# Two steps' 64-row low products on the two halves of the array's rows, in the kernel of an attention and two feed-forward networks

## The chip, the core and the metric

The kernel runs on one core of a Trainium2 chip. TensorE (PE in the rows) multiplies, its weight loads (PEld) stand apart from its matmuls; VectorE is DVE, ScalarE is ACT, GpSimd is POOL, SyncE (SP) issues transfers. The metric is the device time of one execution in microseconds. Before the change the median of three runs is 1066.04 us (1063.58 to 1072.04).

## The reference

Three stages follow each other. The first is a recurrence over 768 steps for 4 x 8 heads of width 40; its output, 3072 rows of 320 numbers, goes through a network of 8 experts (one expert a row, a hidden layer of 1024, relu) and a second network with one set of weights (a hidden layer of 2048, elu). The change touches the two networks alone:

```python
    h = np.maximum(np.einsum('ecd,edf->ecf', disp, w1), 0.0)
    y = np.einsum('ecf,efd->ecd', h, w2)
    ...
    out[i] = gate_w[i] * y[expert_idx[i], pos[i]]
```

```python
    h = x @ w_in
    alpha = 1.0
    g = np.where(h > 0.0, h, alpha * (np.exp(np.minimum(h, 0.0)) - 1.0))
    return (g @ w_out).astype(np.float32)
```

## The kernel before, in words

Every float32 operand of the networks is split into a high part, rounded to the format fp32r, and a low part, what the rounding left. A product is the sum of high by high, low by high and high by low. The input has 320 rows (the contraction), in three pieces of 128, 128 and 64.

A *block* is a set of tokens: 8 blocks of 448 columns for the experts (class `Turned`), then 6 blocks of 512 for the second network (class `Sorted`). A block runs over *steps*, each 128 hidden units: 8 steps for an expert, 16 for the second network, so 64 + 96 = 160 steps in all. In step f the method `s1` makes the hidden layer's product in one bank of PSUM (`ph`) by eight matmuls (L968). Six of them take the pieces of 128 rows: the high and the low weights by the high input `XH`, the high weights by the low input `XL`. The last two take the 64-row piece from the tile `XS`, which has the high input in partitions 0 to 63 and the low input in 64 to 127. The weights of these 64 rows lie twice, in the upper and in the lower partitions, so the high weights `ha` by XS give high by high and high by low at once. The low weights `la` by XS give low by high and, beside it, low by low.

Then `s2` makes the second layer's product of an earlier step (three steps back for an expert, four for the second network) in the banks `po`: 8 matmuls of 448 columns, or 12 of 320 (L992 to L994). After that the activation of the step runs on ACT, DVE and POOL, in two parts that lie a step apart: relu (L1097, L1098), or elu (L1104 to L1112), whose last reader of the bank ph is L1110 on DVE. `run` writes this order out: s1, s2, the activation's parts, a part of the preparation of the next block, then the splitting of weights four groups of steps ahead (ACT L775, POOL L780) and, during the experts, the conversion of the second network's weights on DVE (L858 to L870).

The pool of the banks ph has four buffers, which the transposes of the next expert's input (`pt`) share. `prep` makes XH, XL and XS of the next block: for experts from transposes in PSUM (L952, L953), for the second network from the loaded rows (L1061, L1062). The last step of an expert writes its output through the tile `half`.

Of the kernel before, what the change touches and what calls it, by code (L numbers as in the profile page):

```python
# [8 lines left out]
F32 = mybir.dt.float32  # L9
F32R = mybir.dt.float32r  # L10
# [12 lines left out]
SL = 448  # L23
# [862 lines left out]
def ffn(tc, nc, cst, disp, xt, w1, w2, w32, out, ring, W0, cv):  # L886
# [3 lines left out]
    ap = ctx.enter_context(tc.tile_pool(name="fa", bufs=2))  # L890
    dr = ctx.enter_context(tc.tile_pool(name="fdr", bufs=1, space=DRAM))
    gp = ctx.enter_context(tc.tile_pool(name="fg", bufs=1))
    ps = ctx.enter_context(tc.tile_pool(name="fps", bufs=4, space=PSUM))
# [11 lines left out]
    class Block:  # L905
# [31 lines left out]
        def parts(s):  # L937
            s.XH = ap.tile([128, 2, 512], F32R, tag="XH", name="XH")
            s.XL = ap.tile([128, 2, 512], F32R, tag="XL", name="XL")
            s.XS = ap.tile([128, 512], F32R, tag="XS", name="XS")  # L940
            return [((s.XH[:, k] if k < 2 else s.XS[0:64])[:, 0:s.T], (s.XL[:, k] if k < 2 else s.XS[64:128])[:, 0:s.T]) for k in range(3)]

        def prep(s, P=None):
            for k, (h, l) in enumerate(s.parts()):
                w = (128, 128, 64)[k]
                if P:
                    p = P[k]
                else:
                    p = ps.tile([128, 512], F32, tag="ph", name="pt")
                    for i in range(4):  # L950
                        s.turn(p, i, k)
                nc.scalar.copy(h, p[0:w, 0:s.T])  # L952
                nc.vector.tensor_tensor(l, p[0:w, 0:s.T], h.bitcast(F32), op=ALU.subtract)  # L953
                if k == 2:
                    s.keep(p)
                yield

# [2 lines left out]

        def s1(s, f):
            ha, la, _, _ = s.W.ab(f)
            p = ps.tile([128, 512], F32, tag="ph", name="ph")
            seq = [(w[:, k], x[:, k]) for w, x in ((ha, s.XH), (la, s.XH), (ha, s.XL)) for k in (0, 1)]
            seq += [(ha[:, 2], s.XS), (la[:, 2], s.XS)]
            p = p[:, 0:s.T]
            for i, (l, r) in enumerate(seq):
                nc.tensor.matmul(p, l, r[:, 0:s.T], start=i == 0, stop=i == len(seq) - 1)  # L968
            H = ap.tile([128, 512], F32R, tag="H", name="H", bufs=6)[:, 0:s.T]
            L = ap.tile([128, 512], F32R, tag="L", name="L", bufs=6)[:, 0:s.T]  # L970
            return p, H, L
# [4 lines left out]
        def s2(s, f, HL):  # L976
            if f == 0:
                s.po = s.bank(4)
            for i in range(4):
                s.part(i, f, HL)  # L980
            if f == s.W.nf - 1:
                s.out()
                for i in range(4):
                    s.evict(i)
# [29 lines left out]
    class Turned(Block):  # L1014
# [8 lines left out]
        def s2(s, f, HL):  # L1023
            _, _, hb, lb = s.W.ab(f)
            _, H, L = HL
            if f == 0:
                s.po = s.bank(3)
            first, last = f == 0, f == s.W.nf - 1
            p0, p1, p2 = (p[:, 0:SL] for p in s.po)
            a, b, c = (slice(128 * k, min(128 * k + 128, D)) for k in range(3))  # L1030
            nc.tensor.matmul(p0, hb[:, a], H, start=first, stop=False)
            nc.tensor.matmul(p1, hb[:, b], H, start=first, stop=False)
            nc.tensor.matmul(p0, lb[:, a], H, start=False, stop=False)
            nc.tensor.matmul(p1, lb[:, b], H, start=False, stop=False)
            if not last:
                nc.tensor.matmul(p2, s.W.tail(f), H, start=first, stop=False)
            nc.tensor.matmul(p0, hb[:, a], L, start=False, stop=last)
            nc.tensor.matmul(p1, hb[:, b], L, start=False, stop=last)
            nc.tensor.matmul(p2[0:64], hb[:, c], L, start=False, stop=False)
            if last:  # L1040
                nc.tensor.matmul(p2, s.W.tail(f), H, start=False, stop=True)
                Y, half = s.Y, ap.tile([64, SL], F32, tag="half", name="half", bufs=1)
                if s.G is None:
                    nc.scalar.copy(Y[:, 0], p0)  # L1044
                    nc.vector.tensor_copy(Y[:, 1], p1)
                    nc.scalar.copy(half, p2[64:128])
                    nc.vector.tensor_tensor(Y[0:64, 2], p2[0:64], half, op=ALU.add)
                else:
                    nc.scalar.copy(half, p2[64:128])
                    nc.vector.tensor_tensor(Y[:, 0], p0, s.G, op=ALU.mult)  # L1050
                    nc.vector.tensor_tensor(Y[:, 1], p1, s.G, op=ALU.mult)
                    nc.vector.tensor_tensor(half, p2[0:64], half, op=ALU.add)
                    nc.vector.tensor_tensor(Y[0:64, 2], half, s.G[0:64], op=ALU.mult)
                s.store(Y)

    class Sorted(Block):

        def prep(s, P=None):
            for k, (h, l) in enumerate(s.parts()):
                x = s.X[0:(128, 128, 64)[k], k]  # L1060
                nc.scalar.copy(h, x)  # L1061
                nc.vector.tensor_tensor(l, x, h.bitcast(F32), op=ALU.subtract)  # L1062
                yield

    def soft(s, tag="s"):
# [48 lines left out]
    def gates():  # L1114

        OH = cst["oh"]
        T = lambda nm, sh, dt=F32: gp.tile(sh, dt, tag="g" + nm, name=nm, bufs=1)
        for nm in ("blk", "tmo", "l1"):
            cst[nm] = T(nm, [128, 128], BF)
        set_gates(nc, cst)  # L1120
        m = T("m", [128, 2, 8, 12])
        nc.vector.memset(m, 1.0)
        nc.vector.memset(m[:, :, :, 0:1], 0.0)
        ic = T("ic", [128, 2, 8, 12], BF)
        nc.vector.tensor_tensor_scan(
            out=ic.rearrange("p b e c -> p (b e c)"), data0=m.rearrange("p b e c -> p (b e c)"),
            data1=OH.rearrange("p b e c -> p (b e c)"), initial=0.0, op0=ALU.mult, op1=ALU.add)
        S = T("S", [128, 2, 8], BF)
        nc.vector.tensor_copy(S, ic[:, :, :, 11])
        p = ps.tile([128, 512], F32, tag="ph", name="pg")  # L1130
        p1 = p[:, 0:192]
        nc.tensor.matmul(p1, cst["tmo"], OH.rearrange("p b e c -> p (b e c)"), start=True, stop=False)
        nc.tensor.matmul(p1, cst["blk"], ic.rearrange("p b e c -> p (b e c)"), start=False, stop=True)
        nc.tensor.matmul(p[:, 192:208], cst["l1"], S.rearrange("p b e -> p (b e)"), start=True, stop=False)
        nc.tensor.matmul(p[:, 200:208], cst["ones"], S[:, 0], start=False, stop=True)
        b = T("b", [128, 2, 8])
        nc.vector.tensor_copy(b.rearrange("p b e -> p (b e)"), p[:, 192:208])
        t = T("t", [128, 2, 8, 12])
        nc.vector.tensor_tensor(t, p1.rearrange("p (b e c) -> p b e c", b=2, e=8),
                                b.unsqueeze(3).to_broadcast([128, 2, 8, 12]), op=ALU.add)  # L1140
        nc.vector.scalar_tensor_tensor(out=t, in0=t, scalar=over["cap"], in1=OH, op0=ALU.is_lt, op1=ALU.mult)
        kp = T("kp", [128, 24])
        nc.vector.tensor_reduce(kp.rearrange("p (c b) -> p b c", b=2), t.rearrange("p b e c -> p b c e"), axis=AX.X, op=ALU.add)
        eb0 = T("eb0", [128, 8])
        nc.vector.tensor_scalar(eb0, cst["ebase"], float(-SL), None, op0=ALU.add)
        nc.vector.tensor_tensor(t, OH, eb0.unsqueeze(1).unsqueeze(3).to_broadcast([128, 2, 8, 12]), op=ALU.mult)
        eb = T("eb", [128, 24])
        nc.vector.tensor_reduce(eb.rearrange("p (c b) -> p b c", b=2), t.rearrange("p b e c -> p b c e"), axis=AX.X, op=ALU.add)
        pos, epos = T("pos", [128, 24]), T("epos", [128, 24])
        nc.vector.tensor_tensor(pos, cst["slot"], eb, op=ALU.subtract)  # L1150
        nc.vector.tensor_scalar(pos, pos, float(-SL), None, op0=ALU.add)
        nc.vector.scalar_tensor_tensor(out=epos, in0=eb, scalar=1.0 / 8, in1=pos, op0=ALU.mult, op1=ALU.add)
        return kp, pos, epos
# [205 lines left out]
    def overflow():  # L1359
# [6 lines left out]
        with tc.For_i(1, nr, 1) as r:  # L1366

            kp, pos, epos = gates()
            zr = ap.tile([128, 512], F32, tag="M", name="M")[:, 0:RW]
            nc.vector.memset(zr, 0.0)  # L1370
# [44 lines left out]
    start = over["start"] = ap.tile([128, 6], F32, name="begin", bufs=1)  # L1415
# [72 lines left out]
```

## Time and profile before

| | before |
|---|---|
| median of 3 runs | 1066.04 us |
| the profiled execution: time, and span | 1064.33 us, 1062.6 us |
| granted TensorE clock, mean | 0.941 of full |
| PE busy | 965.8 us (91%), 9995 matmuls |
| PEld busy | 871.9 us (82%) |
| DVE, ACT, POOL busy | 727.8, 516.9, 606.5 us |
| chain that ended last | PE 28%, issue 10%, POOL 6%, DVE 6%; its largest line PE ph L968, 14% |

The attention takes the first 453 us, the experts run to about 690 us, the second network from there on. A row of a timeline gives the start of a group, how long it lasted, the engine, the line, the operation with the tile written and the tiles read, then for PE the rows and columns of the array that it uses (64*64 is a quarter), the operand's shape and the count. Matmuls are pipelined, and their ends are modelled: the time from one start to the next tells what each costs, and the recorded length holds a constant tail. In the rows, fp32r operands are named f32.

### The profile page before, as it was taken

To read this page: it belongs to the slowest core of one execution; us is meant where nothing else is said; L and a number is where in the kernel's file an instruction comes from. 1 tells how busy PE (TensorE), PEld (TensorE's weight loads), DVE (VectorE), ACT (ScalarE), POOL (GpSimd) and SP (SyncE) were. 2 spreads that over 40 slices of the span, in tenths; PEclk is the share of its full clock that TensorE was granted. 3 is DMA by queue.
4 is the path that set the end of the run, shared out by engine and by line. 5 is a ranking of instruction groups with operands and counts; after the bars stand their busy time and mean duration, and the time that the engine had idled before them with its cause. 6 is when DMAs were issued, how large, how long until landed. Compare 5 with 4: busy or idle time off the path is not lost.

```text
span 1062.6 us, 25351 instructions
## 1 busy us (share of the span) xinstructions
PE 965.8 (91%) x9995; PEld 871.9 (82%) x9995; DVE 727.8 (68%) x1287; ACT 516.9 (49%) x1011; POOL 606.5 (57%) x926
## 2 busy tenths in 40 slices
PE   5869978899899999888999999989999999999993
PEld 4758877798788889677889888869989989989983
DVE  8856756788674677549798963656766767776751
ACT  4646544556463334244535545454555455554551
POOL 4757839899898813456677876733323333323332
PEclk9866988899899889999999999989999999999997
DMA  6768675667654864576877765400101010100000
GB/s 165 163 179 197 168 137 105 151 131 141 139 110 103 192 164 103 155 203 168 230 218 209 221 193 188 161 23 3 48 1 32 19 26 25 26 25 1 26 1 28
DMA packets 180984, 121.67 MB, mean 115 GB/s; under 512 B 105792, under 2 KB 166872, under 8 KB 179224
## 3 DMA queue, kind: packets, MB, share of 16 engines
q1 hardware_dynamic: 176788, 102.89, 39.6%
q0 software_dynamic: 3168, 11.14, 3.0%
q10 hardware_dynamic: 900, 5.93, 2.2%
q8 instruction: 81, 1.33, 0.6%
q14 instruction: 47, 0.39, 0.1%
HBM read 86.87 MB, written 33.05 MB: 113 GB/s over the span
## 4 chain that ended last, share of the span: by engine, by line
PE 28%; issue 10%; POOL 6%; DVE 6%; DMA 4%; ACT 2%; SPq 1%; POOLq 0%; DVEq 0%; ACTq 0%
PE ph L968 14%; PE po L992 4%; PE po L994 4%; PE po L993 4%; POOL ring L780 3%; POOL L L1112 2%; DMA ring<-in_w_dram 2%; DVE L L1098 1%; ACT ring L775 1%; SPq L801 1%; DMA S<-in_w_in_dram 1%; DMA w<-E 1%; POOL out_dram L1282 1%; DVE E L859 1%; DVE M L867 1%
## 5 line engine op out<-in xcount | busy, mean ns | idle before, releaser
L780 POOL TENSOR_TENSOR ring<-ring,ring 128x64 fp32r<-128x64 f32 (+2 forms) x320 | 195.7, 647 | 90.0 <-ACT ring L775 87.7
L1112 POOL TENSOR_TENSOR L<-E,H 128x512 fp32r<-128x512 f32 x66 | 87.6, 1327 | 185.8 <-ACT H L1111 148.2
L968 PE MATMUL ph<-XH,ring 128*128 128x512 f32 (+1 forms) x640 | 172.9, 392 | 4.4 <-DVE L L1098 3.9
L968 PEld LDWEIGHTS ph<-XH,ring 128*128 128x128 f32 x640 | 117.4, 193 | 19.6 <-DVE L L1098 4.5
L1105 ACT ACTIVATE E<-N 128x512 f32<-128x512 f32 x96 | 60.7, 633 | 143.7 <-DVE N L1104 88.0
L992 PE MATMUL po<-ring,H 128*128 128x320 f32 x384 | 119.6, 311 | 5.5 <-ACT Y L1044 5.3
L353 POOL TENSOR_TENSOR X<-X,ring 128x60 f32<-128x60 f32 (+19 forms) x170 | 114.9, 676 | 13.3
L994 PE MATMUL po<-ring,L 128*128 128x320 f32 x384 | 119.6, 311 | 1.5 <-POOL L L1112 1.5
L993 PE MATMUL po<-ring,H 128*128 128x320 f32 x384 | 119.4, 311 | 0.0
L1104 DVE TENSOR_SCALAR N<-ph 128x512 f32<-128x512 f32 x96 | 65.9, 686 | 47.4 <-PE ph L968 47.0
L968 PE MATMUL ph<-XL,ring 128*128 128x512 f32 (+1 forms) x320 | 97.6, 386 | 0.0
L968 PE MATMUL ph<-XS,ring 128*128 128x512 f32 (+1 forms) x320 | 97.5, 386 | 0.0
L351 POOL TENSOR_TENSOR ring<-X,ring 128x60 f32<-128x60 f32 (+19 forms) x108 | 74.2, 687 | 39.0 <-DMA ring<-dab 18.2
L992 PEld LDWEIGHTS po<-ring,H 128*128 128x128 f32 x384 | 72.6, 189 | 10.5 <-ACT Y L1044 5.7
L993 PEld LDWEIGHTS po<-ring,H 128*128 128x128 f32 x384 | 72.7, 189 | 4.1
L994 PEld LDWEIGHTS po<-ring,L 128*128 128x128 f32 x384 | 72.9, 190 | 2.0 <-POOL L L1112 2.0
L1109 DVE SCALAR_TENSOR_TENSOR M<-E,M 128x512 f32<-128x512 f32 x96 | 70.7, 736 | 5.5 <-ACT M L1106 5.5
L775 ACT CAST ring<-ring 128x704 fp32r<-128x704 f32 x80 | 61.4, 779 | 21.3 <-issue 8.2
L1110 DVE SCALAR_TENSOR_TENSOR E<-ph,M 128x512 f32<-128x512 f32 x96 | 66.4, 691 | 7.8
L968 PEld LDWEIGHTS ph<-XL,ring 128*128 128x128 f32 x320 | 61.1, 191 | 10.8
L968 PEld LDWEIGHTS ph<-XS,ring 128*128 128x128 f32 x320 | 60.8, 190 | 10.8
L1111 ACT CAST H<-E 128x512 fp32r<-128x512 f32 x96 | 59.2, 617 | 15.1 <-DVE E L1110 12.0
(238 smaller groups left out, 2164.2 us busy)
## 6 DMA issues: line engine op xcount, KB each, us to landing
ring<-in_w_dram SPq DMA_DIRECT2D x16, 640.0 KB
ring<-in_w_dram SPq DMA_DIRECT2D x32, 256.0 KB
RVU<-in_d_in_dram SPq DMA_DIRECT2D x48, 160.0 KB
dab<-AB SPq DMA_DIRECT2D x24, 256.0 KB
ring<-in_e_in_dram ACTq DMA_DIRECT2D x18, 321.6 KB
ring<-w SPq DMA_DIRECT2D x4, 1408.0 KB
disp<-ring SPq DMA_DIRECT2D x8, 575.8 KB
ring<-in_w_dram SPq DMA_DIRECT2D x32, 128.0 KB
```

The lines of the kernel that those rows point to most:

```text
L351: nc.gpsimd.tensor_tensor(tv, X[:, 0:n, s:s + 1].to_broadcast([128, n, m]), N[:, s:s + 1, s + 1:e].to_broadcast([128, n, m]), op=ALU.mult)
L353: nc.gpsimd.tensor_tensor(X[:, 0:n, s + 1:e], X[:, 0:n, s + 1:e], tv, op=ALU.subtract)
L775: s.nc.scalar.copy(B[:, 0:704], r)
L780: s.nc.gpsimd.tensor_tensor(B[:, to], r[:, q], B[:, q].bitcast(F32), op=ALU.subtract)
L968: nc.tensor.matmul(p, l, r[:, 0:s.T], start=i == 0, stop=i == len(seq) - 1)
L992: nc.tensor.matmul(o, H[:, c], hb, start=f == 0, stop=False)
L993: nc.tensor.matmul(o, H[:, c], lb, start=False, stop=False)
L994: nc.tensor.matmul(o, L[:, c], hb, start=False, stop=f == s.W.nf - 1)
L1104: nc.vector.tensor_scalar(N, p, 0.0, None, op0=ALU.min)
L1109: nc.vector.scalar_tensor_tensor(out=M, in0=E, scalar=1.0, in1=M, op0=ALU.add, op1=ALU.mult)
L1110: nc.vector.scalar_tensor_tensor(out=E, in0=p, scalar=0.0, in1=M, op0=ALU.max, op1=ALU.add)
L1112: eng.tensor_tensor(L, E, H.bitcast(F32), op=ALU.subtract)
```

## The change

For each pair of steps (f even, f + 1) `s1` takes both banks ph at the beginning of the even step. The low weights' product of the 64-row piece is no longer a matmul of full height in each step. In the even step the matmul L973 takes the upper 64 partitions alone (low weights by the high input, without low by low), and right behind it L974 does the same for the next step, on the lower 64 partitions, with that step's low weights and a second copy of the high input, `XD`, which stands in partitions 64 to 127. L974 opens the bank of the odd step, whose `s1` then has seven matmuls. `prep` gets one copy more on ACT for XD. To make room for XD, `half` moves into a buffer of the tile N, and a tile t of the gates (run only when an expert overflows) into the tile m.

```diff
             s.XS = ap.tile([128, 512], F32R, tag="XS", name="XS")
+            s.XD = ap.tile([128, 512], F32R, tag="XD", name="XD")
...
                 if k == 2:
+                    nc.scalar.copy(s.XD[64:128, 0:s.T], p[0:64, 0:s.T])
                     s.keep(p)
...
             ha, la, _, _ = s.W.ab(f)
-            p = ps.tile([128, 512], F32, tag="ph", name="ph")
+            if f % 2 == 0:
+                s.ph = [ps.tile([128, 512], F32, tag="ph", name="ph")[:, 0:s.T] for _ in range(2)]
+            p = s.ph[f % 2]
             seq = [(w[:, k], x[:, k]) for w, x in ((ha, s.XH), (la, s.XH), (ha, s.XL)) for k in (0, 1)]
-            seq += [(ha[:, 2], s.XS), (la[:, 2], s.XS)]
-            p = p[:, 0:s.T]
+            seq += [(ha[:, 2], s.XS)]
             for i, (l, r) in enumerate(seq):
-                nc.tensor.matmul(p, l, r[:, 0:s.T], start=i == 0, stop=i == len(seq) - 1)
+                nc.tensor.matmul(p, l, r[:, 0:s.T], start=f % 2 == 0 and i == 0, stop=f % 2 == 1 and i == len(seq) - 1)
+            if f % 2 == 0:
+                nc.tensor.matmul(p, la[0:64, 2], s.XS[0:64, 0:s.T], start=False, stop=True)
+                nc.tensor.matmul(s.ph[1], s.W.ab(f + 1)[1][64:128, 2], s.XD[64:128, 0:s.T], start=True, stop=False)
...
-                Y, half = s.Y, ap.tile([64, SL], F32, tag="half", name="half", bufs=1)
+                Y, half = s.Y, ap.tile([128, 512], F32, tag="N", name="N")[0:64, 0:SL]
...
+                if k == 2:
+                    nc.scalar.copy(s.XD[64:128], x)
...
-        t = T("t", [128, 2, 8, 12])
+        t = T("m", [128, 2, 8, 12])
```

What this does to the order on TensorE is shown at two places. The first is the beginning of the first expert, steps 0 and 1, before the change (ph is the hidden layer's bank, ring_5566 the weights):

```order
L968 MATMUL ph<-XH,ring_5566 128x448 x4
L968 MATMUL ph<-XL,ring_5566 128x448 x2
L968 MATMUL ph<-XS,ring_5566 128x448 x2
L968 MATMUL ph<-XH,ring_5566 128x448 x4
L968 MATMUL ph<-XL,ring_5566 128x448 x2
L968 MATMUL ph<-XS,ring_5566 128x448 x2
```

And the same two steps after it:

```order
L971 MATMUL ph<-XH,ring_5566 128x448 x4
L971 MATMUL ph<-XL,ring_5566 128x448 x2
L971 MATMUL ph<-XS,ring_5566 128x448
L973 MATMUL ph<-XS,ring_5566 128x448
L974 MATMUL ph<-XD,ring_5566 128x448
L971 MATMUL ph<-XH,ring_5566 128x448 x4
L971 MATMUL ph<-XL,ring_5566 128x448 x2
L971 MATMUL ph<-XS,ring_5566 128x448
```

The even step has kept eight matmuls and got a ninth, which belongs to the odd step; the odd step has seven. The second place is an even step of the second network with the beginning of the s2 that follows it (po is an output bank), before and then after the change:

```order
L968 MATMUL ph<-XH,ring_8868 128x512 x4
L968 MATMUL ph<-XL,ring_8868 128x512 x2
L968 MATMUL ph<-XS,ring_8868 128x512 x2
L992 MATMUL po<-ring_8793,H 128x320
L993 MATMUL po<-ring_8793,H 128x320
L994 MATMUL po<-ring_8793,L 128x320
```

```order
L971 MATMUL ph<-XH,ring_8886 128x512 x4
L971 MATMUL ph<-XL,ring_8886 128x512 x2
L971 MATMUL ph<-XS,ring_8886 128x512
L973 MATMUL ph<-XS,ring_8886 128x512
L974 MATMUL ph<-XD,ring_8886 128x512
L998 MATMUL po<-ring_8811,H 128x320
L999 MATMUL po<-ring_8811,H 128x320
L1000 MATMUL po<-ring_8811,L 128x320
```

L973 and L974 stand between the last full-height matmul of s1 and the first of s2 (L998, which was L992). The order on the other engines is as it was, with the copy XD added on ACT behind the cast of XS.

## Rows read from the trace of the kernel before

**Rows 1.** Windows by stage: length, busy us by engine (count), clock, DMA, GB/s.
```profile
core 0: us, PE busy (x) PEld busy (x) DVE busy (x) ACT busy (x) POOL busy (x), PEclk, DMA share, GB/s
453.00:709.00 256.00, 238.58 (x1167) 209.98 (x1166) 179.60 (x323) 125.05 (x231) 175.70 (x286) 0.97 0.65 187
709.00:1062.60 353.60, 337.07 (x1865) 303.62 (x1863) 229.14 (x335) 174.56 (x304) 115.83 (x117) 0.98 0.06 20
```
**Rows 2.** Waits of PE, 453 to 709 us: total us, times, longest us.
```profile
PE po L992 <- ACT Y L1044: 5.3, 1, 5.3
PE ph L968 <- DVE L L1098: 3.9, 2, 3.4
PE po L1031 <- DVE Y L1050: 2.6, 1, 2.6
```
**Rows 3.** Waits of PE, 709 us to the end.
```profile
PE po L994 <- POOL L L1112: 1.5, 2, 0.8
```
**Rows 4.** Timeline of PE in a step of the second network.
```profile
803.87 0.63 PE L968 MATMUL ph<-XS,ring 128*128 128x512 f32 x2
804.34 0.30 PE L992 MATMUL po<-ring,H 128*128 128x320 f32 x1
```
**Rows 5.** Timeline of PE in a step of an expert.
```profile
562.33 0.58 PE L968 MATMUL ph<-XS,ring 128*128 128x448 f32 x2
562.75 0.36 PE L1031 MATMUL po<-H,ring 128*128 128x448 f32 x1
```
**Rows 6.** Timeline of PEld, the load ahead of that L992.
```profile
804.11 0.19 PEld L992 LDWEIGHTS po<-ring,H 128*128 128x128 f32 x1
```
**Rows 7.** Timeline of PE and PEld, 314.60 to 314.63 us: full height to quarters.
```profile
314.41 0.28 PE L525 MATMUL q<-RVU 128*128 128x128 f32 x1
314.62 0.27 PE L469 MATMUL ut<-TT,RH 64*64 64x64 f32 x2
314.62 0.14 PEld L469 LDWEIGHTS ut<-TT,RH 64*64 64x64 f32 x2
```
**Rows 8.** The same, 315.72 to 315.75 us: quarters to full height.
```profile
315.54 0.22 PE L469 MATMUL ut<-TT,RH 64*64 64x64 f32 x2
315.70 0.38 PE L525 MATMUL q<-RVU 128*128 128x128 f32 x1
315.70 0.19 PEld L525 LDWEIGHTS q<-RVU 128*128 128x128 f32 x1
```
**Rows 9.** The same, 151.955 to 151.97 us: rows change, columns don't.
```profile
151.75 0.28 PE L469 MATMUL ut<-TT,RH 64*64 64x64 f32 x4
151.96 0.14 PEld L539 LDWEIGHTS y<-RVU,SD 128*64 128x64 f32 x2
```
**Rows 10.** The same, 560.42 to 560.52 us: columns change, rows don't.
```profile
560.30 0.36 PE L1038 MATMUL po<-L,ring 128*128 128x448 f32 x1
560.31 0.14 PEld L1039 LDWEIGHTS po<-L,ring 128*64 128x64 f32 x1
```
**Rows 11.** Timeline of PE, quarters in pairs and halves by columns.
```profile
314.62 1.15 PE L469 MATMUL ut<-TT,RH 64*64 64x64 f32 x32
318.21 1.10 PE L539 MATMUL y<-RVU,SD 128*64 128x128 f32 x16
```
**Rows 12.** Groups by line and shape, PE: count, busy us, mean ns, idle before.
```profile
L968 PE MATMUL ph<-XS,ring 128*128 128x512 f32 x192 | 60.5, 396 | 0.0
L968 PE MATMUL ph<-XS,ring 128*128 128x448 f32 x128 | 37.0, 371 | 0.0
```
**Rows 13.** The same, ACT, 453 to 1062 us.
```profile
L1061 ACT CAST XS<-X 64x512 fp32r<-64x512 f32 x6 | 3.7, 616 | 0.0
```
**Rows 14.** Timeline of DVE at two places.
```profile
477.44 0.43 DVE L858 TENSOR_SCALAR N<-S 128x512 int32<-128x512 int32 x1 [7.41 <-DMA S<-in_w_in_dram]
797.05 0.69 DVE L1110 SCALAR_TENSOR_TENSOR E<-ph,M 128x512 f32<-128x512 f32 x1
```
**Rows 15.** Timeline of PE, end of the s1 three steps later.
```profile
800.25 0.62 PE L968 MATMUL ph<-XS,ring 128*128 128x512 f32 x2
```

## The prediction

> **What bounds the kernel now.** I read the table of windows first, then the waits of the tensor engine, then single matmuls. The change touches only the two networks, which run from about 453 us to the end. There the matmul engine is busy 238.6 of 256.0 us and 337.1 of 353.6 us [rows 1], and its waits name little else: the longest of the expert stage is 5.3 us, once, the next 3.9 us in two [rows 2]; the third stands at 2.6 us, and from 709 us on there is 1.5 us in all, at the very end [rows 2, 3]. So every tenth of a microsecond that a step gains or loses on this engine shows in the time nearly whole, in the second network above all.
>
> A step of the second network gives 0.47 us to its last two matmuls, the two on XS: 803.87 to 804.34, so 0.235 us each [rows 4]. In an expert the two take 562.33 to 562.75, 0.21 us each [rows 5]. Each also needs a load of weights; but the load for the next matmul starts at 804.11 [rows 6], as soon as the matmul ahead of it (803.87 + 0.235) has begun, and so lies wholly beside it. That is the cover to keep in mind.
>
> **What goes and what comes.** Two steps now have four XS matmuls of full height; afterwards they have two of full height and two of 64 rows, L973 and L974, which are meant to run side by side. There are as many instructions as before: 192 XS matmuls of 512 columns (2 for each of 96 steps) and 128 of 448 (64 steps) [rows 12]. If a pair took the time of one matmul and nothing else happened, 48 pairs x 0.225 and 32 x 0.20 would go (0.01 us for the later start of the second): 10.8 + 6.4 = 17.2 us.
>
> **Do two halves run together?** The attention has pairs on opposite quarters of the array. Their records start together (the two of "314.62 0.27 x2" share a start), and 32 of them, 16 pairs, span 1.15 us, against 1.10 us for 16 matmuls twice as wide [rows 7, 11]. So yes for quarters that share neither rows nor columns. The new pair shares all 128 columns and writes two banks; no row shows that. Bounds: 0.01 us for the second, or its whole slot (0.235 and 0.21). I take 0.01, since the nearest rows are of that kind.
>
> **What the change of height costs.** Here the rows speak against the change. The last full-height matmul ahead of such quarters starts at 314.41 and is recorded for 0.28; the first load of quarter size starts only at 314.62, 0.07 before that recorded end, not 0.01 after the matmul's start as usual [rows 7]. On the way back it is the same: last quarters at 315.54 for 0.22, the next load at 315.70, 0.06 before their end [rows 8]. Where only the rows change (64 high and 64 wide to 128 high and 64 wide) it stays: 151.75 + 0.28, less 151.96, is 0.07 [rows 9]. Where only the columns change, 128 wide to 64 wide, the load follows its matmul at once, 560.30 and 560.31 [rows 10]. Nor is a semaphore the likely cause: the lag is the same 0.06 to 0.07 at all three places, whoever produces the next operand. So a change of the number of rows empties the engine, and the loads behind it lose their cover: the first full matmul after it is recorded for 0.38 instead of 0.28, 0.10 us in which its weights arrive; for quarters it is 0.27 against 0.22, 0.05 [rows 7, 8].
>
> The Trainium skill, TensorEngine Tiling (Array Packing), section Tiling Modes, says the same: a change of the tiling mode, not just of the tile, drains the engine. It gives no figure; the trace agrees with it by the 0.07 and 0.10 above.
>
> Now the sum for two steps, from the start of the last full-height XS matmul of the even step. At 512 columns a matmul is recorded for 0.40 (0.63 for two, less 0.235) [rows 4]: load at 0.40 - 0.07 = 0.33, stream from 0.43, second half 0.01 later, load of the next full matmul 0.33 after that at 0.77, its stream at 0.87. Before, that stream began at 0.47. So the even step loses 0.40, the odd one, an XS matmul shorter, gains 0.235: a loss of 0.165 a pair, 48 x 0.165 = 7.9 us. At 448 columns (recorded 0.37): 0.30, 0.40, 0.41, 0.71, 0.81 against 0.42 [rows 5]; 0.39 - 0.21 = 0.18 a pair, 32 x 0.18 = 5.8 us. Together 13.7 us more.
>
> Bounds: the first load has half the rows, so its uncovered part may be 0.05 as for quarters: 80 x 0.05 = 4.0 less. The lag I read to 0.02, twice a pair: 3.2 either way.
>
> **What hides some of it.** In the second network no wait is left to take it up. In the experts there is. At 477.44 VectorE gets a transfer after 7.41 us of idleness [rows 14], and the tensor engine's longest wait on VectorE's L (3.4 of the 3.9) hangs on that; what is late by less before it costs nothing: steps 0, 2, 4 and 6, four pairs. The waits of 2.6 and 5.3 us should swallow some seven more. 11 x 0.18 = 2.0 us less; the bounds are 0 and all 5.8. I take 2.0, because the other waits follow chains that the tensor engine's own steps feed, so they move along.
>
> **The rest.** The bank of an odd step is opened a half step earlier, so its last reader must be done earlier. In the second network the reader of three steps ahead ends at 797.05 + 0.69 = 797.74, and the place of the new L974 is 800.25 + 0.235 = 800.49: 2.7 us of room [rows 14, 15]. So nothing; without this room each pair would wait. The low weights that L974 takes belong to the next step of the same group and are split by POOL well ahead. The copy XD is one more cast of the size of XS's (0.616 us in each of the 6 blocks of the second network, and one for each of the 8 experts) [rows 13]; ACT is busy 125 of 256 us and 175 of 354 us [rows 1], and the copy is needed only a step later: nothing; if it had to be waited for, 14 x 0.6 = 8 us. `half` takes a buffer of N, which VectorE has long left: nothing. The gates' t in m runs only in the overflow loop.
>
> Sum: 13.7 - 2.0 = 11.7 us over the profiled execution's 1064.33: 1076.0. The median of the three runs is 1.7 higher (1066.04), and by it the sum is 1077.7. I predict **1077 us**.
>
> **Rivals.**
> - **No stop (1047 us).** The array stays 128 columns wide and the engine lets loads of half height pass as it lets those of half width pass [rows 10]. Then the 17.2 us of the second paragraph are won: 1064.3 - 17.2. Against it stand both ways of changing rows [rows 7, 8] and the row-only case [rows 9]. It decides as soon as a stop with its uncovered loads is under 0.1 us a change. Chance 0.08. The Trainium skill, TensorE: Matmul & The Clock Gate, Part 3 (packing small matmuls), counts such a pack as one matmul plus some 4 ns for each further tile; taken alone it gives this case, an estimate of 17.6 us won. No row of before shows 64 rows with all 128 columns.
> - **Halves in sequence.** The pair shares its columns and runs one after the other: 48 x 0.235 + 32 x 0.21 = 18.0 more, 1094 us. Chance 0.09.
> - **A bank not free.** In the experts other tiles use the banks too and VectorE's readers stand behind conversions, so an opening may wait there by about 1 us a block: 7 us, 1083 us. Chance 0.08.
> - **The forecast**, own range from 1065 (13.7 - 4.0 - 3.2 - 5.8 = 0.7) to 1081 (16.9): 0.75.
>
> **How the numbers follow.** The range has to hold 8 in 10: the forecast (0.75) and the bank's case (0.08) lie within 1065 to 1088 but for their tails; halves in sequence and no stop, 0.17 together, are left out. One per cent (10.7 us) is about what a measurement here can tell from no change. The forecast lies just above it, by 0.55 of its chance: slower 0.75 x 0.55 + 0.09 + 0.07 = 0.57; faster 0.08; same the rest, 0.35.
>
> **What would show it.** L973 and L974 starting within 0.02 us, the load of L973 some 0.33 us behind the start of the XS matmul ahead, the load of the next po matmul as far behind L974; the first po matmul recorded 0.10 longer; even steps of the second network 0.40 us longer than now, odd ones 0.235 shorter. If L974 starts 0.2 later than L973, the halves run in sequence; if the load of L973 stands 0.24 behind the XS matmul's start, there is no stop and I am wrong by sign. A wait of L974 on VectorE's L or E is the bank.

## The result and the profile after

The changed kernel takes 1078.43 us (median of 19 runs, 1071.66 to 1083.11); the kernel before, beside it, 1066.04 us (19 runs, 1059.64 to 1072.95). The ratio is 1.0115, with a 95% interval of 1.0097 to 1.0133: 12.3 us longer, 10.3 to 14.2. The profiled execution of the changed kernel has 1078.43 us and a span of 1076.6.

| | before | after |
|---|---|---|
| median, us | 1066.04 | 1078.43 |
| profiled execution, span, us | 1064.33, 1062.6 | 1078.43, 1076.6 |
| PE busy, us | 965.8 | 978.7 |
| PEld busy, us | 871.9 | 848.1 |
| mean granted clock | 0.941 | 0.945 |

The first view is the timeline of the tensor engine (PE matmuls, PEld weight loads) in an even and an odd step of the second network after the change; the columns are start, duration, engine, line, operation, tiles, rows*columns of the array, shape, count, and in brackets the idle time ahead. Line numbers here and below are each kernel's own. The view answers to [rows 4, 6].

```profile
816.65 0.40 PE L971 MATMUL ph<-XS,ring 128*128 128x512 f32 x1
816.98 0.18 PEld L973 LDWEIGHTS ph<-XS,ring 64*128 64x128 f32 x1 [0.36 <-issue]
816.98 0.49 PE L973 MATMUL ph<-XS,ring 64*128 64x512 f32 x1
816.98 0.18 PEld L974 LDWEIGHTS ph<-XD,ring 64*128 64x128 f32 x1
816.98 0.49 PE L974 MATMUL ph<-XD,ring 64*128 64x512 f32 x1
817.40 0.19 PEld L998 LDWEIGHTS po<-ring,H 128*128 128x128 f32 x1 [0.24 <-issue]
817.41 0.41 PE L998 MATMUL po<-ring,H 128*128 128x320 f32 x1
817.51 0.19 PEld L999 LDWEIGHTS po<-ring,H 128*128 128x128 f32 x1
...
820.65 0.40 PE L971 MATMUL ph<-XS,ring 128*128 128x512 f32 x1
820.65 0.19 PEld L998 LDWEIGHTS po<-ring,H 128*128 128x128 f32 x1
820.89 0.31 PE L998 MATMUL po<-ring,H 128*128 128x320 f32 x1
```

The reader is to see three things. The two halves start together (816.98 and 816.98). The load for L973 does not follow at the start of the XS matmul (816.65), as the load for L998 does in the odd step (820.65), but 0.33 us behind it; and the load for the first po matmul stands 0.42 us behind that of the halves. A load that stands alone shows in the length of its matmul: the first po matmul is recorded for 0.41 instead of 0.30 us. The load after it (L999) starts when the stream of that matmul does, at 817.51, so the even step needs 0.86 us from its XS matmul to that stream, where a step before needed 0.47 [rows 4]; the odd step needs 0.24. The lines by shape say the same of all steps (count | busy us, mean ns of one | idle ahead); they answer to [rows 12]:

```profile
L998 PE MATMUL po<-ring,H 128*128 128x320 f32 x384 | 124.3, 324 | 1.4 <-ACT Y L1050 1.2 <-ACT H L1119 0.2
L973 PE MATMUL ph<-XS,ring 64*128 64x512 f32 x48 | 23.7, 493 | 0.0
L974 PE MATMUL ph<-XD,ring 64*128 64x512 f32 x48 | 23.6, 491 | 3.5 <-DVE E L1118 3.5
L973 PE MATMUL ph<-XS,ring 64*128 64x448 f32 x32 | 15.5, 484 | 0.0
```

The Trainium skill, TensorEngine Tiling (Array Packing), section Tiling Modes, says that a change of the mode drains the engine; this trace agrees, on the way in by 0.33 and on the way out by 0.42 us. A change of the columns alone, to 64 and back in an experiment below, emptied nothing (3.627 us a step against 3.622); if that rule is meant for such a change too, the measurement decides. The Trainium skill, TensorE: Matmul & The Clock Gate, Part 3, prices a pack at one matmul and about 4 ns for each further tile; the common start of the halves agrees with that, and the way in and out, which the formula leaves out, is what decided here.

The waits of the tensor engine after 453 us (total us, times, longest) answer to [rows 2, 3]:

```profile
PE ph L971 <- DVE L L1106: 4.2, 1, 4.2
PE ph L974 <- DVE E L1118: 3.5, 1, 3.5
PE po L1043 <- DVE L L1106: 2.3, 1, 2.3
PE po L1000 <- POOL L L1120: 1.5, 2, 0.8
PE po L998 <- ACT Y L1050: 1.2, 1, 1.2
```

The wait of L974 for a bank occurs once (beside one of 0.2 us in the experts), and the wait of the po matmul on ACT's Y, 5.3 us before [rows 2], is 1.2: it is the same hold-up at the entry to the second network, met one matmul earlier. From the XS matmul ahead to that po matmul it is 5.94 us after the change and 5.93 before.

And by windows (length, busy us by engine, granted clock, DMA share, GB/s), which answers to [rows 1]:

```profile
453.00:709.00 256.00, 241.21 (x1152) 196.10 (x1150) 175.49 (x313) 124.82 (x231) 172.09 (x279) 0.98 0.65 185
709.00:1076.60 367.60, 349.51 (x1880) 296.71 (x1880) 231.37 (x345) 182.38 (x318) 121.83 (x125) 0.97 0.07 21
```

The granted clock is 0.98 and 0.97, where it was 0.97 and 0.98 [rows 1]: the loss is not one of the clock.

### The profile page after: what moved, and what is told of

It reads as the page before. It is cut to its first block, busy times and chain, and to the rows that moved or that the text cites. A ratio compares the mean times of both kernels' runs of the same rounds, so it can differ in the third digit from the quotient of the medians.

```text
span 1076.6 us, 25407 instructions
## 1 busy us (share of the span) xinstructions
PE 978.7 (91%) x9995; PEld 848.1 (79%) x9995; DVE 724.6 (67%) x1287; ACT 524.7 (49%) x1025; POOL 607.8 (56%) x926
## 3 DMA queue, kind: packets, MB, share of 16 engines
q10 hardware_dynamic: 900, 5.93, 2.1%
## 4 chain that ended last, share of the span: by engine, by line
issue 25%; POOL 12%; DVE 8%; PE 6%; DMA 4%; ACT 2%; SPq 1%; POOLq 0%; ACTq 0%; DVEq 0%
POOL L L1120 8%; PE ph L971 2%; POOL out_dram L1290 2%; POOL ring L780 2%; DMA w<-E 2%; DVE L L1106 2%; DMA ring<-in_w_dram 1%; DVE E L859 1%; DMA S<-in_w_in_dram 1%; ACT ring L775 1%; DVE N L869 1%; DVE M L867 1%; DVE N L858 1%; SPq L801 1%; DVE M L865 0%
## 5 line engine op out<-in xcount | busy, mean ns | idle before, releaser
L353 POOL TENSOR_TENSOR X<-X,ring 128x60 f32<-128x60 f32 (+19 forms) x170 | 119.6, 704 | 13.3
L998 PE MATMUL po<-ring,H 128*128 128x320 f32 x384 | 124.3, 324 | 1.4 <-ACT Y L1050 1.2
L999 PE MATMUL po<-ring,H 128*128 128x320 f32 x384 | 119.5, 311 | 0.0
L351 POOL TENSOR_TENSOR ring<-X,ring 128x60 f32<-128x60 f32 (+19 forms) x108 | 72.0, 666 | 38.1 <-DMA ring<-dab 17.4
L998 PEld LDWEIGHTS po<-ring,H 128*128 128x128 f32 x384 | 72.8, 190 | 14.8 <-issue 7.2
L999 PEld LDWEIGHTS po<-ring,H 128*128 128x128 f32 x384 | 72.9, 190 | 2.1
L1117 DVE SCALAR_TENSOR_TENSOR M<-E,M 128x512 f32<-128x512 f32 x96 | 67.9, 707 | 2.8 <-ACT M L1114 2.8
L971 PE MATMUL ph<-XS,ring 128*128 128x512 f32 (+1 forms) x160 | 62.1, 388 | 0.0
L1106 DVE SCALAR_TENSOR_TENSOR L<-ph,H 128x448 fp32r<-128x448 f32 x64 | 39.4, 617 | 33.5 <-ACT H L1105 33.5
```

The source lines that it names most:

```text
L351: nc.gpsimd.tensor_tensor(tv, X[:, 0:n, s:s + 1].to_broadcast([128, n, m]), N[:, s:s + 1, s + 1:e].to_broadcast([128, n, m]), op=ALU.mult)
L353: nc.gpsimd.tensor_tensor(X[:, 0:n, s + 1:e], X[:, 0:n, s + 1:e], tv, op=ALU.subtract)
L971: nc.tensor.matmul(p, l, r[:, 0:s.T], start=f % 2 == 0 and i == 0, stop=f % 2 == 1 and i == len(seq) - 1)
L998: nc.tensor.matmul(o, H[:, c], hb, start=f == 0, stop=False)
L999: nc.tensor.matmul(o, H[:, c], lb, start=False, stop=False)
L1117: nc.vector.scalar_tensor_tensor(out=M, in0=E, scalar=1.0, in1=M, op0=ALU.add, op1=ALU.mult)
```

## The experiments

All medians are compared with the kernel before on the same chip; the difference in us is the ratio's distance from 1 times the median of before, with its 95% interval.

**Is it the height, or what came with it?** The banks, the copy and the order stay as changed; only the height goes back:

```diff
-                nc.tensor.matmul(p, la[0:64, 2], s.XS[0:64, 0:s.T], start=False, stop=True)
-                nc.tensor.matmul(s.ph[1], s.W.ab(f + 1)[1][64:128, 2], s.XD[64:128, 0:s.T], start=True, stop=False)
+                nc.tensor.matmul(p, la[:, 2], s.XS[:, 0:s.T], start=False, stop=True)
+                nc.tensor.matmul(s.ph[1], s.W.ab(f + 1)[1][:, 2], s.XS[:, 0:s.T], start=True, stop=False)
```

> The changed kernel with its order, its banks, the copy XD and `half` in N, but L973 and L974 as matmuls of full height: the low weights' product of both steps stands in the even step, 128 rows high, one behind the other. Theory (the changes of height are the whole loss): the four XS matmuls of a pair take 4 x 0.235 us again, the loads lie beside them, and the time is that of the kernel before, 1066 us, within 3. Rival (the bank opened a step early, the copy or the other moves cost it): the loss stays, 1075 us or more, since nothing of these was taken back. In the trace the load behind the even step's first XS matmul should start 0.24 us after the load of that matmul, not 0.33 us behind its stream's start, and the first po matmul should be recorded for 0.31 as before, not 0.32 with an uncovered load.

Measured: 1064.93 against 1064.66 us, +1.2 (-1.5 to 3.8). The timeline of that kernel at the same place:

```profile
814.42 0.39 PE L971 MATMUL ph<-XS,ring 128*128 128x512 f32 x1
814.42 0.19 PEld L973 LDWEIGHTS ph<-XS,ring 128*128 128x128 f32 x1
814.65 0.39 PE L973 MATMUL ph<-XS,ring 128*128 128x512 f32 x1
814.65 0.19 PEld L974 LDWEIGHTS ph<-XS,ring 128*128 128x128 f32 x1
814.88 0.39 PE L974 MATMUL ph<-XS,ring 128*128 128x512 f32 x1
814.88 0.19 PEld L998 LDWEIGHTS po<-ring,H 128*128 128x128 f32 x1
815.11 0.31 PE L998 MATMUL po<-ring,H 128*128 128x320 f32 x1
```

Every load starts with the matmul ahead, and the streams follow each other at 0.23 us. So the early bank, XD and `half` cost no more than 3.8 us together, and the loss needs the 64 rows. Its profile shows the bank's wait all the same (L974 on E, 3.6 us, once), at no cost that the time shows.

**Do the halves run together, and what does a second pair cost?** One kernel drops L974, and the odd step's own first matmul opens its bank again; another issues the pair twice:

```diff
...
             if f % 2 == 0:
                 nc.tensor.matmul(p, la[0:64, 2], s.XS[0:64, 0:s.T], start=False, stop=True)
-                nc.tensor.matmul(s.ph[1], s.W.ab(f + 1)[1][64:128, 2], s.XD[64:128, 0:s.T], start=True, stop=False)
```

> The changed kernel without L974: the even step keeps its 64-row matmul and so both changes of height, the odd step's low weights of the last 64 rows are left out, and its bank is opened by its own first matmul. Theory (the two halves run beside each other, the stop is the price): 80 x 0.01 us less at most, 1077 to 1078 us. Rival (the second half takes a slot of its own, hidden in the records): 48 x 0.235 + 32 x 0.21 = 18.0 us less, 1060 us. Rival (the bank opened early costs): less by the waits of L974 in the trace, 3.7 us, 1074.5 us.

Measured: 1077.22 against 1064.66 us, +13.6 (10.6 to 16.6), as the changed kernel's +12.3. Half the work gone, nothing gained: the second half is free. In the trace an even step of the second network takes 1.006 us with one half and 1.004 with two (medians, from its XS matmul to the second po matmul).

```diff
+                nc.tensor.matmul(p, la[0:64, 2], s.XS[0:64, 0:s.T], start=False, stop=False)
+                nc.tensor.matmul(s.ph[1], s.W.ab(f + 1)[1][64:128, 2], s.XD[64:128, 0:s.T], start=True, stop=False)
                 nc.tensor.matmul(p, la[0:64, 2], s.XS[0:64, 0:s.T], start=False, stop=True)
-                nc.tensor.matmul(s.ph[1], s.W.ab(f + 1)[1][64:128, 2], s.XD[64:128, 0:s.T], start=True, stop=False)
+                nc.tensor.matmul(s.ph[1], s.W.ab(f + 1)[1][64:128, 2], s.XD[64:128, 0:s.T], start=False, stop=False)
```

> The changed kernel with the two 64-row matmuls issued twice in a row, so that the same two products enter twice: four halves between one entry and one return. Theory (the price is in the changes of height, the halves themselves run two by two at a matmul's length): 48 x 0.225 + 32 x 0.20 = 17 us over the changed kernel, 1094 us, the third half starting 0.22 us behind the second. Rival (halves that share the columns are slow themselves): 30 us or more over the changed kernel, 1108 us. Rival (the second pair loads and streams under the first, so that the stop covers part of it): 10 us or less, under 1088 us.

Measured: 1087.04 against 1065.41 us, +20.0 (15.0 to 25.1), so 8 over the changed kernel (a difference of two comparisons, some 5 us either way) and not 17. By this number alone the rival in which the stop covers part of the second pair would hold (under 1088 us); the trace decides (L975 and L976 are the second pair):

```profile
815.89 0.40 PE L971 MATMUL ph<-XS,ring 128*128 128x512 f32 x1
...
816.22 0.49 PE L973 MATMUL ph<-XS,ring 64*128 64x512 f32 x1
...
816.33 0.19 PEld L975 LDWEIGHTS ph<-XS,ring 64*128 64x128 f32 x1
...
816.55 0.39 PE L975 MATMUL ph<-XS,ring 64*128 64x512 f32 x1
816.56 0.39 PE L976 MATMUL ph<-XD,ring 64*128 64x512 f32 x1
...
816.88 0.41 PE L1000 MATMUL po<-ring,H 128*128 128x320 f32 x1
```

Inside half height no stop occurs: the loads of the second pair (816.33) lie beside the first, and the po matmul stands 0.66 us behind the first half instead of 0.42. That is 0.24 a pair, as expected, and 48 x 0.24 = 11.5 us; the second network takes 12.3 us longer than in the changed kernel (table below), so the stop covers nothing of the second pair. In an expert too the second pair adds 0.20 us (1.204 against 1.001, medians from the XS matmul to the second po matmul), but the length of the expert stage shows none of these 32 x 0.20 = 6.4 us, and its gaps are smaller by some 5 (table below): that part of the expectation failed, and the same failure comes back in the next runs.

**Rows or columns, and twice as many stops?** Each step has its own low matmul ahead of its XS matmul, either 64 rows high or 64 columns wide (the other 64 hidden units' low product is left out):

```diff
...
+                if i == len(seq) - 1:
+                    nc.tensor.matmul(p, la[0:64, 2], s.XS[0:64, 0:s.T], start=False, stop=False)
...
+                if i == len(seq) - 1:
+                    nc.tensor.matmul(p[0:64], la[:, 2, 0:64], s.XS[:, 0:s.T], start=False, stop=False)
```

> No pairs: every step has its own 64-row matmul of its low weights, placed ahead of its full-height XS matmul (the low weights' product with the low half of XS is left out, as in the changed kernel), so 160 entries into half height and 160 returns instead of 80 and 80, and no second bank opened early. Theory (each entry and return empties the engine and leaves a load uncovered): 0.40 us a step at 512 columns and 0.39 at 448 over the kernel before, 96 x 0.40 + 64 x 0.39 = 63 us, 1128 us. Rival (the loss comes from pairs and banks, not from height): at most a few us over the kernel before, 1065 to 1070. Rival (only the entry or only the return costs): half, 1097 us.

> The same place in each step, but the low weights' matmul is 128 rows high and 64 columns wide (the other 64 hidden units' low product is left out): only the number of columns changes, 160 times in and out. Theory (columns don't empty the engine, the load follows at once): as long as a full matmul, 0.235 and 0.21 us, so the time of the kernel before, 1065 us, within 4. Rival (any change of size empties it): 63 us more, 1128 us. In the trace the load behind it should start about 0.24 us after its own load, against 0.33 behind the matmul ahead for rows.

Measured: rows 1112.22 against 1065.41 us, +47.4 (42.1 to 52.8); columns 1067.80, +3.5 (0.6 to 6.5). First the rows' trace, then that of the columns:

```profile
817.73 0.18 PEld L972 LDWEIGHTS ph<-XS,ring 64*128 64x128 f32 x1 [0.36 <-issue]
...
818.15 0.19 PEld L973 LDWEIGHTS ph<-XS,ring 128*128 128x128 f32 x1 [0.25 <-issue]
818.16 0.50 PE L973 MATMUL ph<-XS,ring 128*128 128x512 f32 x1
818.26 0.19 PEld L997 LDWEIGHTS po<-ring,H 128*128 128x128 f32 x1
```

```profile
814.94 0.14 PEld L972 LDWEIGHTS ph<-XS,ring 128*64 128x64 f32 x1
815.17 0.39 PE L972 MATMUL ph<-XS,ring 128*64 128x512 f32 x1
815.17 0.19 PEld L973 LDWEIGHTS ph<-XS,ring 128*128 128x128 f32 x1
815.40 0.40 PE L973 MATMUL ph<-XS,ring 128*128 128x512 f32 x1
```

With half the columns every load starts beside the matmul ahead; with half the rows it waits on the way in and on the way out, at the same 0.42 us between the two loads. A step of the second network takes 4.007 us with rows and 3.627 with columns (medians from start to start; 3.622 before). The 0.385 a step are 37.0 us in 96 steps, close to the 38.4 expected, and the stage is some 36.4 us longer. The experts should have given 25 and gave some 6 to 12: 246.0 us, against 234.5 to 240.5 with the matmuls of before (table below). The 3.5 us of the columns are not in the second network (363.7 us there, 363.3 to 363.6 before); where they are is not shown.

**Where it is paid: one network at a time.** `Turned`, or `Sorted`, keeps the method `s1` of the kernel before; the rest is as changed (XD stays in the experts of the first of these kernels):

```diff
     class Turned(Block):
+        def s1(s, f):   # as in the kernel before
```

> The change in the second network alone: the experts multiply as before, each step with its own full-height low weights (the copies XD stay). Theory: 48 pairs x 0.155 to 0.165 us = 7.4 to 7.9 us over the kernel before, 1073.5 to 1074 us; what is left to the changed kernel's 1078.4, 4.5 to 5 us, is the experts' part, so that they swallowed about 1 us of 5.8. Rival (the experts' part was swallowed as forecast, 3.8 us left): the second network alone would have to give 8.6 us, 1074.6. Rival (the loss sits in the experts by banks and waits): under 1070 us.

> The change in the experts alone (32 pairs of 448 columns, XD and `half` there as in the changed kernel); the second network as before, without XD. Theory with the forecast's own terms: 32 x 0.18 = 5.8 us gross, less the 2.0 us that waits should swallow, 3.8 us over the kernel before. Theory without that swallowing: 5.8 us. Rival (the experts are paced by other engines, as the small gain of the kernel with the odd low weights left out suggests): 2 us or less, since the changed kernel stood 1.15% and the one changed in the second network alone 0.96% above the kernel before, a difference of 2 us.

Measured: the second network alone 1074.90 against 1064.66 us, +10.2 (7.5 to 13.0); the experts alone 1066.99 against 1065.41, +0.6 (-2.2 to 3.5). Most of the loss lies in the second network. The 5.8 us of the experts with nothing swallowed lie outside the interval, and so, by a little, do the 3.8 of the forecast. Taken the other way, the changed kernel stands 2.1 us above the one with the second network alone (12.3 against 10.2), but some 3.4 either way, which does not rule the 3.8 out.

**What a pair would give if nothing stopped.** Three kernels leave low products out and change no height: the odd steps' in both networks, the odd steps' in the second network alone, and all of them.

```diff
...
-                nc.tensor.matmul(p, la[0:64, 2], s.XS[0:64, 0:s.T], start=False, stop=True)
-                nc.tensor.matmul(s.ph[1], s.W.ab(f + 1)[1][64:128, 2], s.XD[64:128, 0:s.T], start=True, stop=False)
+                nc.tensor.matmul(p, la[:, 2], s.XS[:, 0:s.T], start=False, stop=True)
```

The second of them gives `Turned` the method of before besides; the third has neither of the two lines, so that every step ends its bank with the XS matmul.

> As the changed kernel, but the even step's low weights' product at full height and that of the odd step left out (no L974): what a pair in the time of one matmul would give if no height changed. Theory: 48 x 0.235 + 32 x 0.21 = 18.0 us under the kernel before, 1048 us, or a little above where waits of the experts take some of it; so the stops cost the changed kernel some 30 us, 0.38 us a pair, against 18 us saved. Rival (the engine is not the bound of these stages): 1060 us or more, and then the loss of the changed kernel could not be the tensor engine's alone.

> The odd steps' low weights of the last 64 rows left out in the second network alone (the even step's at full height), the experts multiply as before. Theory A: 48 x 0.235 = 11.3 us under the kernel before, 1054 us. Theory B (as the trace of the kernel with both networks so cut shows: 56.8 us for 16 steps instead of 58.0, a wait of 0.56 us at each block's start, and the last block longer): 4 to 7 us less, 1058 to 1061 us.

> The low weights' product of the last 64 rows left out in every step of both networks: seven matmuls in the first half of a step, no change of height. Theory A (the tensor engine is the bound of both networks): 96 x 0.235 + 64 x 0.21 = 36 us under the kernel before, 1029 us. Theory B (it is the bound in the second network alone; the experts are paced by weights, conversions and the other engines, so a gain there is lost in waits): about 22 us less from the second network at most, nearly nothing from the experts, 1043 to 1050 us, with the tensor engine's idle time in the expert stage some 10 us above the 12 of the kernel before. Where it is near 1060, both stages are held by others.

Measured, in this order: 1062.17 us, -1.9 (-4.6 to 0.6); 1061.89, -3.4 (-6.8 to 0.0); 1061.61, -4.2 (-6.8 to -1.6). Against 18, 11.3 and 36 us of matmuls that are gone, next to nothing is won: my theory failed here, by its own number of 1048, and for the last of them theory B was still too hopeful with 1043 to 1050; for the second its 4 to 7 us less lie within the interval. The longest waits of the kernel without any of these products, first up to 700 us, then from 709 to 1035 us:

```profile
PE po L1035 <- DVE Y L1048: 8.4, 4, 3.1
PE ph L971 <- DVE L L1103: 7.2, 3, 5.2
PE po L1040 <- DVE L L1103: 4.0, 1, 4.0
```

```profile
PE po L995 <- DVE Y L1007: 9.1, 5, 2.0
```

Before, nothing of the last kind stood among the waits [rows 2, 3]. Now the first po matmul of each later block of the second network waits up to 2.0 us until VectorE has copied the block ahead out of its bank. The two timelines at one such place, VectorE and then PE:

```profile
822.13 0.69 DVE L1117 TENSOR_TENSOR L<-E,H 128x512 fp32r<-128x512 f32 x1 [0.74 <-ACT H L1116]
...
822.81 0.88 DVE L1007 COPY Y<-po 128x320 f32<-128x320 f32 x2
```

```profile
820.99 0.40 PE L971 MATMUL ph<-XS,ring 128*128 128x512 f32 x1
823.44 0.38 PE L995 MATMUL po<-ring,H 128*128 128x320 f32 x1 [2.05 <-DVE Y L1007]
```

The copies stand behind a conversion (L1117) that itself waits 0.74 us for ACT's H. It waits so in the kernel before too; what differs is how late the chain of VectorE and ACT runs. Before, the copies at such a place were done 1.5 us ahead of the next block's first po matmul, and VectorE often waited for the tensor engine's ph. The copies and that matmul before, and then VectorE's wait for ph between 715 and 1030 us, before and in this kernel:

```profile
820.06 0.88 DVE L1004 COPY Y<-po 128x320 f32<-128x320 f32 x2
822.46 0.31 PE L992 MATMUL po<-ring,H 128*128 128x320 f32 x1
```

```profile
DVE N L1104 <- PE ph L968: 41.4, 37, 1.5
DVE N L1109 <- PE ph L971: 14.1, 14, 1.4
```

With most of that slack used up the chain keeps its own pace, and a faster tensor engine only meets it earlier. Part of the rest went into slower matmuls: the windows of this kernel show a granted clock of 0.96 in both networks, against 0.97 and 0.98 before [rows 1], in stretches in which the engine waits more:

```profile
453.00:709.00 256.00, 225.82 (x1074) 195.05 (x1073) 177.67 (x316) 126.70 (x233) 172.35 (x282) 0.96 0.65 184
709.00:1062.10 353.10, 326.62 (x1789) 294.46 (x1787) 227.64 (x341) 175.96 (x313) 121.62 (x121) 0.96 0.07 21
```

Worked out from the traces, the 96 x 0.235 = 22.6 us that are gone from the second network went as follows: its length is 6.1 us shorter, the gaps between its matmuls are 10.2 us longer (17.2 against 7.0), and the clock stood at its lower level (1.2 GHz) for 17.1 us instead of 6.8, which can cost half of the difference, some 5 us, at most.

**How far one profile of a stage can be trusted.** Both kernels were profiled a second time.

> The kernel before once more, for a second profile: how much the length of a stage differs from one execution to the next. If the expert stage (243.4 us from its first matmul of step 0 to that of step 64) and the second network (354.5 us) repeat within 1 us, the 6.9 and 6.6 us by which the changed kernel's profile is longer in them stand each by itself; if the expert stage moves by several, as the profiles of the other kernels suggest (246 to 249 us where its matmuls are as before), its share of the loss can't be read from one profile.

> The changed kernel once more, for a second profile. The second network should repeat its 29.6 us for 8 steps and 361.0 us in all to 0.5 us. The expert stage (250.3 us) should come out lower, 247 to 249 us, if the first profile was at the upper end of its spread; at 250 or more, the experts do lose 6 us.

Those executions took 1064.34 and 1076.29 us. The table, worked out from the timelines, goes from the start of the first matmul on XH of 448 columns to that of 512 columns (experts), and on to the start of the last matmul (second network); idle is the sum of the gaps between PE's matmul records in the experts. The lengths that the expectations of these two runs give for the stages go from and to other steps, so only differences compare.

| kernel | experts, us | idle there | second network, us |
|---|---|---|---|
| before, two profiles | 234.5, 236.5 | 12.1, 12.6 | 363.3, 363.6 |
| full height, same order | 237.1 | 14.5 | 362.8 |
| columns in each step | 238.4 | 15.5 | 363.7 |
| second network alone | 239.2 | 13.6 | 371.1 |
| experts alone | 238.0 | 9.7 | 363.8 |
| after, two profiles | 240.9, 237.7 | 11.9, 10.5 | 370.4, 370.2 |
| one half | 239.8 | 11.1 | 370.4 |
| two pairs | 237.2 | 6.4 | 382.7 |
| rows in each step | 246.0 | 3.7 | 399.9 |
| odd low left out | 236.1 | 16.6 | 359.0 |
| odd low left out, second network | 240.5 | 15.6 | 356.9 |
| all low left out | 241.4 | 24.7 | 357.3 |

The second network repeats within 1 us where its matmuls are unchanged; the experts move by 6 us (234.5 to 240.5) with the same matmuls, and by 2.0 and 3.2 us between two profiles of one kernel. So the 6.4 us by which the first profile after was longer in the experts say little: the second one was 1.2 us longer than its counterpart. The kernels with the experts' matmuls of before but with the copy XD and `half` in N lie at 237.1 to 240.5, above both profiles of before: a part of the 6 us may be these edits, which the run at full height bounds at 3.8 us in all. The idle time says more: the engine's gaps shrink from 12 to 16 us to about 10 to 12 with the change, to 6.4 with two pairs, to 3.7 with rows in each step, and grow to 24.7 with all low products left out. The gaps take up what the engine loses and what it wins.

## Why the prediction was right, and where it was not

The forecast, 1077 us and slower, came out at 1078.43. The parts, in its order:

- **A change of height empties the engine: right, shown.** Forecast load 0.33 behind the XS matmul and next stream at 0.87, measured 0.33 and 0.86; 0.41 us recorded for the first po matmul, 0.10 longer as said. The next load was to stand 0.33 behind L974 and stands 0.42 behind its recorded start, which holds the uncovered load (0.49 us recorded instead of 0.39). With the height taken back the loss is gone, with columns in its place there are no stops, and with a stop in every step the second network pays 0.385 us for each (0.40 forecast).
- **The halves run together: right, shown,** by their common start and by the kernel with one half, which is not faster. The rival of halves in sequence falls.
- **The loss for a pair: right.** At 512 columns 16 steps take 59.25 us against 58.0 (starts of the same step in successive blocks), 0.156 a pair where 0.165 was forecast, 7.5 us in 48 pairs against 7.9; the stage is 6.6 to 7.1 longer, its gaps a little smaller. At 448 columns an even step takes 0.395 us more from its XS matmul to the second po matmul (medians, 1.001 against 0.606) and an odd one 0.196 less (0.410): 0.20 a pair where 0.18 was forecast, 6.4 us in 32 pairs against 5.8. The experts' length without gaps says it more coarsely: 227.2 to 229.0 us in the three profiles with the change, 222.4 to 225.5 in the five with the experts' matmuls of before.
- **What waits swallow: the term of 2.0 us was mis-sized.** The experts alone cost 0.6 us (-2.2 to 3.5), not 3.8: of some 6 us most vanished, though the interval leaves anything from all of it to some 2.5 us. I had counted single waits of [rows 2] that hang on one late transfer and taken the others to move along with the engine. But the kernel with rows in each step shows that 8 to 9 of the 12 us of gaps can be filled: its experts have 3.7 left. That the gaps are where the loss went is read from these sums, not from single waits.
- **The rest at nothing: right within 3.8 us.** The bank's wait exists once and replaces an older one; the rival of a wait in every block falls.
- **"Every tenth of a microsecond that a step gains or loses shows nearly whole": half wrong.** It holds for losses in the second network. For gains it fails in both networks, and with it the price of the rival without a stop: not 17.2 us under the kernel before (1047), but 1.9 (-0.6 to 4.6), by the kernel that leaves the odd products out. That rival could not have come about by its stated condition alone. The rows that should have warned were at hand: VectorE busy 229 of 354 us [rows 1], and its copies at the blocks' ends, done only 1.5 us before the matmul that needs their bank.

The sum is closer than its terms, and that it came so close is partly luck. Second network 6.8, experts about 1, the other edits 1.2 (-1.5 to 3.8) make some 9 of the 12.3 us (10.3 to 14.2). What the missing 3 us are is open: the attention, which the change does not touch, ends between 445.8 and 452.4 us in these profiles, and that and the experts' spread hide as much; the other edits may hold some of it, within their 3.8 us.

## What to carry to other kernels

Half-height matmuls in pairs save a matmul's time only inside a run of them: here the way in and out costs 0.39 us, a pair saves 0.225, and a second pair between the same ends costs only 0.24. By these numbers two pairs between the same two changes of height would about break even (an estimate; no run replaced four full matmuls so), and more of them could gain. A matmul of half the columns changed nothing around it, so a change of columns has no such price; whether two halves by columns run beside each other at 512 columns no run here shows. Before pricing a gain on the busiest engine, look for the chain that has no wait on it now and will be met next; the gaps on the engine can swallow a loss, that chain limits a gain, and the two are not the same number. A stage whose length moves by 6 us between executions of the same matmuls can't be judged from one profile; its gaps and a kernel changed in that stage alone can.

## What the runs showed of the hardware

- Two halves by rows that share all 128 columns and write two banks start together (816.98 and 816.98) and are done in the time of one: no row of before had shown it.
- The load of a half is recorded for 0.18 us against 0.19 for a full one, so fewer rows made the uncovered load no shorter (for half the columns it is 0.14).
- Between half-height matmuls the loads go ahead as usual (816.33, 0.11 us behind the start of the pair ahead, in the kernel with two pairs); the stop is tied to the change alone.
- Where all low products were left out and the tensor engine had more gaps, its granted clock was lower: 0.933 over the whole execution, the mean of ten (0.925 to 0.941), against 0.940 in the 17 of the kernel before beside it (0.931 to 0.948). One of the five waits for VectorE's copies was followed by a stretch at the lower level (1.2 GHz), behind the other four the clock stayed at 2.4: part of what is won can come back as slower matmuls. The windows of that kernel around this wait, with 3.04 us busy of the 5 ahead of it:

```profile
875.00:880.00 5.00, 3.04 (x17) 2.38 (x15) 3.81 (x8) 2.73 (x6) 0.00 (x0) 1.00 0.00 0
880.00:885.00 5.00, 4.92 (x19) 4.54 (x20) 4.25 (x8) 2.44 (x5) 4.22 (x7) 0.66 0.27 98
```
